# Attention and gated MLP in one kernel: two exponentials of a step joined over two PSUM banks, unit maxima turned by VectorE, other engines for small copies

## The chip, the cores and the metric

The kernel runs on one core of a Trainium2 chip. The metric is the device time of one execution in microseconds (us), lower is better. A core has TensorE (PE; its weight loads are shown apart as PEld), VectorE (DVE), ScalarE (ACT), GpSimd (POOL) and SyncE (SP, which here only issues DMAs). Matmuls write to PSUM, eight banks of 128 partitions x 512 float32.

## What is computed

Shapes: x is 2048 x 512, 32 heads of 16, the MLP has 1376 hidden columns. All is float32.

```python
xn = _layernorm(x, axis=-1)
s = _A_ref(xn, A_wqkv, A_wo)          # multi-head attention: softmax(q k^T / 4) v, then @ wo
g = _silu(_B_ref(xn, B_w1, B_b1, B_w2, B_b2))   # gelu(xn @ w1 + b1) @ w2 + b2
return x + s * g
```

## The kernel before, in words

The work is done in stages. First x is normalised and turned, V and the first of Q and K are projected (to about 60 us). Then the MLP and the other projections run (60 to 466 us). Then comes attention (466 to about 1540 us), and the output projection with the gate, which is interleaved with the last part of attention.

Attention is cut into 32 *units*, u = 4g + c: a group g of four heads and a chunk c of 512 queries. A unit has 16 *steps*, one for each block k of 128 keys. There are two kinds of score matmuls.

- **S, the scores for the row maxima** (`s_whole`, `s_op`, L185). Queries lie on the partitions, keys along 512 columns; VectorE takes maxima of each half of the bank with one reduction (`s_max`, L191, output `mx`). A unit needs 64 of these banks. A third of them is made ahead, during the MLP (`fill`, LEAD = 144 of each kind), so that attention starts with nine units of maxima in hand; in attention three are made a step.
- **T, the scores for the exponentials** (`t_one`, L715). Keys lie on the partitions, the unit's 512 queries along the columns, with two more contraction rows that carry minus the row maximum in two parts. ScalarE makes the exponential (L717, output `PT[u, k]`, one 128 x 512 block for each of the four heads). Then four matmuls of 32 columns each, in pieces that show as eight rows, multiply by V (`pv_step`, L781) into one bank, `pv`, kept through the 16 steps of the unit. L781 of step n uses the exponentials of step n - 1.

Each step issues a fixed sequence, a string in `ORDER` or `AFTER`: T is a score matmul for an exponential, S a whole bank of scores for maxima, X and Y the two halves (256 columns each) of a bank that is filled by both row halves of the array, V is L781. Before Y, PE's queue holds until the matmul of X has ended. The letter strings are chosen by the step's place k in its unit. When maxima are used up, for the last 20 steps, the string is "TTTTV", with output projection matmuls (L905) between.

Score matmuls have 48 or 50 contraction rows, so two fit on the array at once: an index `a` of 0 or 1 gives the row half (partitions 0 or 64 on). The program is in manual order: each engine works through its instructions as they were emitted. The first S of a step is on half 0, the second on half 1; X is on half 0, Y on half 1. The four T of a step have (p, a) = (0, 1), (1, 1), (0, 0), (1, 0).

PSUM: `ps_a`, `ps_b` and `ps_x` form a ring for S, X and Y (`s_tile`). T uses `ps_m` and the three rotating banks of `ps_t` (`t_tile`), `pv` has `ps_v`.

The way of the maxima of a unit: 64 reductions fill `mx`; `s_end0` reduces it with a sign change to `nm`, 128 queries x 16 (L248); Pool splits `nm` into a high and a low part (L251, L252); `s_end1` turns both, for two units together (a *pair*, up to unit 28), by a matmul with an identity into a bank (L268); `s_end2` copies that to SBUF, by ScalarE during the MLP and by VectorE later (L276, L278), and sends it to DRAM with one DMA (L279). `load_mh` brings it back as the two extra rows of Q (L153). `s_end0` is called only in the steps with k > 2 of a unit, and from unit 28 on at once. The turn follows two calls of V later in attention.

At the end of a unit, one V into the next, VectorE copies `pv` to `os` (L788) and DMAs spread it (L801, L804); division by the sum follows with Pool (L819). `pv` has one bank, so the V of the next unit's first step waits for that copy.

Of the kernel before, what the change touches and what calls it, by code (L numbers as in the profile page):

```python
# [40 lines left out]
ORDER = {0: "TTTTV", 3: "TSXTTSTYV"}  # L41
AFTER = {0: "STXTTSTYV", 2: "XTSTTYSTV"}
HC = CH // 2
PAIRED = 28
KB = 3
# [5 lines left out]
def fused(ctx: ExitStack, tc: tile.TileContext, x, wqk, wv, wo, w1, b1, w2, b2, out):  # L51
# [7 lines left out]
    ps_t = ctx.enter_context(tc.tile_pool(name="ps_t", bufs=3, space=PSUM))  # L59
# [8 lines left out]
    mh_d = dpool.tile([NG * NCH, 2, GH, CH], F32, name="mh_d")  # L68

    ident_r = keep.tile([P, P], F32R, name="ident_r")  # L70
# [16 lines left out]
    QS, QT, MX, NM, MH = {}, {}, {}, {}, {}  # L87
# [62 lines left out]
    def load_mh(u):  # L150
        assert u in sent
        for a in range(2):
            nc.sync.dma_start(QT[u][64 * a + 48:64 * a + 50].bitcast(F32), mh_d[u, :, a::2, :])  # L153
# [13 lines left out]
    def flush():  # L167
        while later and later[0][0] <= 0:
            u = later.pop(0)[1]
            run_off()  # L170
            s_end1(u)
            s_end2(u)
# [65 lines left out]
    def s_end0(u):  # L238
        ended.remove(u)
        nm = qring.tile([P, GH * NCH], F32, name="nm")  # L240
        n = len(units_of(u))
        if u == units_of(u)[0]:
            NM[u] = qring.tile([P, 2, 2, GH * NCH], F32R, name="nmh")[:, :n]
        hl = NM[units_of(u)[0]][:, u % n]
        if u == units_of(u)[-1]:
            later.append([12 if "seen" in prog else 8, units_of(u)[0]])
        mx = MX.pop(u).rearrange("p a b c n -> p (a b) (c n)")
        nc.vector.tensor_reduce(nm, mx, axis=AX.X, op=OP.max, negate=True)  # L248

        def two():  # L250
            nc.gpsimd.tensor_copy(hl[:, 0], nm)  # L251
            nc.gpsimd.tensor_sub(hl[:, 1], nm, hl[:, 0].bitcast(F32))  # L252

        put_off.append(two)
        if "seen" in prog or u == NU - 1:
            run_off()
        del QS[u]
        if "seen" in prog:
            ask_qs(u + 2)
        else:  # L260
            load_qs(u + 2)
# [3 lines left out]
    def s_end1(u):  # L265
        pm = s_tile()[0] if "seen" in prog or u == NU - 1 else t_tile()
        n = 2 * GH * NCH * len(units_of(u))
        nc.tensor.matmul(pm[:n, :P], NM.pop(u).rearrange("p u i a -> p (u i a)"), ident_r, start=True, stop=True)  # L268
        MH[u] = pm

    def s_end2(u):
        us = units_of(u)
        n = 2 * GH * NCH * len(us)
        mh = qring.tile([4 * GH * NCH, P], F32, name="mh", bufs=1)
        if "seen" in prog:
            nc.scalar.activation(mh[:n], MH.pop(u)[:n, :P], AF.Copy)  # L276
# [115 lines left out]
    with ExitStack() as s1:  # L392
# [4 lines left out]
        def a_tile(shape):  # L397
# [4 lines left out]
            return ps_t.tile(list(shape), F32, name="pst")  # L402
# [77 lines left out]
        def consts():  # L480
# [4 lines left out]
            nc.gpsimd.tensor_copy(ident_r, ident)  # L485
# [55 lines left out]
    new_k(keep_r)  # L541
    kts.append([kv[:, p] for p in range(2)])
# [17 lines left out]
    s_when, put, row = [], [0], [0]  # L560
    def fill(a):
        due = 2 * FILL0 + APART * (put[0] + sum(made))
        if sum(made) < 4 * LEAD and row[0] >= due and (made[0] <= made[1]) == (a == 0):
            taken()
            if later and later[0][0] <= 0:
                put[0] += 1
                u = later.pop(0)[1]
                s_end1(u)
                s_end2(u)
                return  # L570
# [54 lines left out]
    def down(c, f, part):  # L625
        i = c * FT + f
        if f == 0 and part == 0:
            PA[c] = [ps_v.tile([P, D], F32, name="pv")] + [ps_t.tile([P, D], F32, name="pst") for t in range(3)]
# [49 lines left out]
    def quad(n, at):  # L678
        us = first[n]
        for u, b in zip(us, BANKS[n]) if at == 0 else ():  # L680
            pool, name = {"x": (ps_x, "ps"), "m": (ps_m, "ps"), "v": (ps_v, "pv"), "t": (ps_t, "pst")}[b]
            PH[u] = pool.tile([P, CH], F32, name=name)
# [15 lines left out]
    turns, PN = [0], []  # L698

    def t_tile():  # L700
        turns[0] += 1
        if turns[0] < 5:
            pool = (ps_m, ps_x, ps_a, ps_b)[turns[0] - 1]
        else:
            pool = ps_m if turns[0] % 4 == 1 else ps_t
        return pool.tile([P, CH], F32, name="pst" if pool is ps_t else "ps")

    def t_one(u, k, p, a):
        g = u // NCH
        if (u, k) not in PT:  # L710
            PT[u, k] = slot(3 + len(PN) % 3, (P, GH, CH))
            PN.append(1)
        ps = t_tile()
# [3 lines left out]
        nc.scalar.activation(PT[u, k][:, 2 * p + a, :], ps, AF.Exp, scale=SCALE)  # L717

    k_ones(kts[0])
    for n, e in enumerate(plan):  # L720
# [6 lines left out]
        else:  # L727
            if e[1] == parts[-2]:
                nc.scalar.activation(mhw, ident_r[:1, :1].bitcast(F32), AF.Exp)
            if e[1] == parts[-1]:  # L730
                for i in range(EARLY):
                    t_one(0, 0, i // 2, i % 2)
# [42 lines left out]
    def pv_step(u, k):  # L775
# [8 lines left out]
        if k == NT - 1:  # L784
            OS[u] = wb.tile([P, CH], F32, name="os", bufs=1)
            pv = PV.pop(u)
            if u < NU - 1:
                nc.vector.tensor_copy(OS[u], pv)  # L788
# [80 lines left out]
    def w_mul(t, ks, parts=(0, 1)):  # L869
        if t not in PW:  # L870
            PW[t] = [ps_t.tile([P, CH], F32, name="pst") if NW <= t < NT - NCH or i else
# [62 lines left out]
    for u in range(NU):  # L934
# [41 lines left out]
    for n in range(L + 1):  # L976
# [78 lines left out]
```

## Time and profile before

| | before |
|---|---|
| median of 3 runs | 1565.8 us (1565.47 to 1566.19) |
| the profiled execution | 1565.5 us |
| its span, first to last instruction | 1563.7 us |
| granted TensorE clock | 1.0 throughout |
| attention, first to last start of V | 470.4 to 1541.3 us |
| maxima reductions on VectorE (L191) | 2048, 687 ns each |
| exponentials on ScalarE (L717) | 2048, 603 ns each |

A profile row gives a line of the program, an engine, an operation, what is written and read (`out<-in`, buffer numbers left out), shapes as partitions x elements, and a count. A weight load shows columns as "128*32". Rows of the timeline begin with the start in us from the span's start and the duration; neighbours of one kind are merged, with "x3" for three. Rows of the sums by stage give the stretch, its length, and for each engine the busy time and the number of instructions. Busy time of PE overlaps itself, because matmuls are pipelined: a row of 0.39 us does not hold the array for 0.39 us. Two rows of the same kind that follow each other give the better price, by the distance of their starts.

### The profile page before, as it was taken

The numbers are of one execution on the slowest core, as the hardware profiler recorded it, in microseconds if no ns is written. First come the engines' busy times: TensorE is split into PE (matmuls) and PEld (weight loads), VectorE is DVE, ScalarE is ACT, GpSimd is POOL, SyncE is SP. The second block draws the span as 40 slices with busy tenths as digits, with TensorE's granted clock in tenths as the row PEclk, the third lists the DMA queues.
The fourth block names the chain that finished last, engine by engine and source line by source line (L and its number), as shares of the span: only waits on it lengthen the run. The fifth ranks groups of instructions, "written<-read, shape, count | busy, mean of one in ns | idle before, by whom it ended". The sixth has DMA issues, their size and how long they took to land.

```text
span 1563.7 us, 31870 instructions
## 1 busy us (share of the span) xinstructions
PE 1556.6 (100%) x12264; PEld 951.5 (61%) x12264; DVE 1416.1 (91%) x2290; ACT 1234.5 (79%) x2397; POOL 371.7 (24%) x394
## 2 busy tenths in 40 slices
PE   9999999999999999999999999999999999999998
PEld 7899999999994444444444444444444444444455
DVE  7599999999999999999999999999999999999834
ACT  4333333434349999999999999999999999999984
POOL 4145575756640011001100100100010000000143
PEclk9999999999999999999999999999999999999999
DMA  6626343454322113111511411321151111110163
GB/s 209 153 60 158 116 139 100 155 145 136 124 91 60 40 42 61 29 38 44 86 24 28 70 41 32 59 44 29 26 79 27 33 29 33 40 30 22 46 197 115
DMA packets 74648, 116.87 MB, mean 75 GB/s; under 512 B 23013, under 2 KB 24293, under 8 KB 73321
## 3 DMA queue, kind: packets, MB, share of 16 engines
q1 hardware_dynamic: 70748, 101.89, 23.9%
q0 software_dynamic: 3264, 12.35, 4.7%
q8 instruction: 97, 1.59, 0.4%
q10 hardware_dynamic: 484, 0.60, 0.1%
q14 instruction: 55, 0.44, 0.1%
HBM read 84.35 MB, written 25.97 MB: 71 GB/s over the span
## 4 chain that ended last, share of the span: by engine, by line
PE 98%; DVE 1%; ACT 0%; DMA 0%; issue 0%; DVEq 0%
PE pv L781 33%; PE pst L715 20%; PE ps L589 13%; PE ps L185 11%; PE pst L589 7%; PE ps L715 7%; PE pv L589 2%; PE ps L905 1%; PE ps L82 1%; PE ps L459 1%; PE pst L82 1%; DVE st L418 0%; PE pst L441 0%; DMA xt<-in_x 0%; PE pst L459 0%; ACT slot L717 0%
## 5 line engine op out<-in xcount | busy, mean ns | idle before, releaser
L191 DVE TENSOR_REDUCE mx<-ps 128x2 f32<-128x512 f32 x2048 | 1317.9, 687 | 87.2 <-PE ps L185 44.4
L717 ACT ACTIVATE slot<-pst 128x512 f32<-128x512 f32 x1533 | 826.0, 603 | 12.8 <-PE pst L715 7.0
L781 PE MATMUL pv<-slot,vsb 128*32 128x512 f32 x4096 | 545.4, 605 | 0.3 <-DVE os L788 0.3
L715 PE MATMUL pst<-qt,kt 50*128 50x512 f32 x1149 | 378.8, 430 | 0.5 <-DVE gt L648 0.3
L185 PE MATMUL ps<-kt,slot 48*128 48x512 f32 (+1 forms) x1364 | 377.1, 368 | 0.0
L715 PEld LDWEIGHTS pst<-qt,kt 50*128 50x128 f32 x1149 | 192.3, 185 | 252.5 <-ACT slot L717 235.9
L717 ACT ACTIVATE slot<-ps 128x512 f32<-128x512 f32 x515 | 310.9, 604 | 1.8 <-PE ps L185 0.7
L185 PEld LDWEIGHTS ps<-kt,slot 48*128 48x128 f32 x1364 | 226.6, 184 | 39.4 <-DVE mx L191 35.4
L589 PE MATMUL ps<-slot,w1h 64*128 64x512 f32 x1088 | 218.4, 393 | 0.0
L185 PE MATMUL ps<-kt,qz 48*128 48x512 f32 x512 | 201.8, 394 | 0.0
L185 PE MATMUL ps<-slot,slot 48*128 48x512 f32 (+1 forms) x598 | 165.3, 366 | 0.0
L715 PE MATMUL ps<-qt,kt 50*128 50x512 f32 x387 | 160.6, 417 | 0.0
L589 PEld LDWEIGHTS ps<-slot,w1h 64*128 64x128 f32 x1088 | 151.9, 186 | 10.5
L589 PE MATMUL ps<-slot,w1l 64*128 64x512 f32 x544 | 148.4, 393 | 0.0
L781 PEld LDWEIGHTS pv<-slot,vsb 128*32 128x32 f32 x4096 | 81.0, 108 | 98.9 <-issue 90.4
L378 POOL TENSOR_TENSOR hl<-hg,hh 128x512 fp32r<-128x512 f32 x76 | 96.8, 1296 | 151.9 <-ACT hh L377 113.9
L251 POOL CAST nmh<-nm 128x16 fp32r<-128x16 f32 x32 | 6.3, 197 | 519.4 <-DVE nm L248 418.0
L371 ACT ACTIVATE hg<-ps,b_sb 128x512 f32<-128x512 f32 x44 | 27.9, 684 | 125.2 <-PE ps L589 100.4
L715 PE MATMUL pst<-qt,slot 50*128 50x512 f32 x384 | 112.5, 416 | 0.0
L185 PEld LDWEIGHTS ps<-slot,slot 48*128 48x128 f32 x598 | 99.1, 184 | 16.4 <-DVE mx L191 15.1
L715 PEld LDWEIGHTS ps<-qt,kt 50*128 50x128 f32 x387 | 71.3, 185 | 41.8 <-ACT slot L717 36.0
L185 PEld LDWEIGHTS ps<-kt,qz 48*128 48x128 f32 x512 | 94.0, 184 | 0.5
(165 smaller groups left out, 1722.6 us busy)
## 6 DMA issues: line engine op xcount, KB each, us to landing
raw<-in_w SPq DMA_DIRECT2D x88, 256.0 KB
qk_h<-hh SPq DMA_DIRECT2D x32, 256.0 KB
qk_l<-hl SPq DMA_DIRECT2D x32, 256.0 KB
qt<-qk_h SPq DMA_DIRECT2D x128, 64.0 KB
slot<-qk_h SPq DMA_DIRECT2D x92, 64.0 KB
g_d<-gt POOLq DMA_DIRECT2D x16, 256.0 KB, 3.4
qt<-qk_l SPq DMA_DIRECT2D x64, 64.0 KB
dn<-den_d SPq DMA_DIRECT2D x32, 128.0 KB
```

The source lines that it names most:

```text
L82: nc.tensor.matmul(ps, lhs[a], rhs[b], start=first and n == 0, stop=last and n == 2)
L185: return nc.tensor.matmul(ps[:, c0:c0 + w], QS[u][r, p, qi * P:(qi + 1) * P], kts[u // NCH % KB][p][r, k0:k0 + w], start=True, stop=True).ins
L191: nc.vector.tensor_reduce(MX[u][:, 2 * p:2 * p + 2, qi, ki][:, heads, parts], ps.rearrange("p (n c) -> p n c", c=HC), axis=AX.X, op=OP.max)
L251: nc.gpsimd.tensor_copy(hl[:, 0], nm)
L371: nc.scalar.activation(raw, ph.pop(u), AF.Gelu_apprx_tanh, bias=b1_sb[:, u[2]:u[2] + 1])
L378: nc.gpsimd.tensor_sub(hl, raw, hh.bitcast(F32))
L459: nc.tensor.matmul(pq["q", g, c], W1[g][i][:, k * P:(k + 1) * P], (xh, xl)[j][c][:, k], start=n == 0 and k == 0, stop=n == 2 and k == KT - 1)
L589: i = nc.tensor.matmul(ps, lhs[r], rhs[r], start=first, stop=last).ins
L715: nc.tensor.matmul(ps, kts[g % KB][p][r, k * P:(k + 1) * P], QT[u][r, p, :], start=True, stop=True)
L717: nc.scalar.activation(PT[u, k][:, 2 * p + a, :], ps, AF.Exp, scale=SCALE)
L781: nc.tensor.matmul(PV[u][32 * j:32 * j + 32, :], vsb[:, k, h:h + 32], PT[u, k][:, j, :], start=(k == 0), stop=(k == NT - 1))
L905: HALF[0] = nc.tensor.matmul(PW[i][0], OTS[i, k][x][r], (wo_h, wo_l)[y][r, k], start=k == 0 and side == 0 and n == 0, stop=k == KT - 1 and ...
```

## The change

- The four T of a step have other sides, `SIDES`: (p, a) = (1, 1), (0, 0), (0, 1), (1, 0). The banks are fixed by the place in the step: the first T has the one bank of `ps_t`, the second and third have the two banks of one tile `two_t`, the fourth has `ps_m`.
- In steps with three S the exponentials of the second and third T are one instruction over both banks, 128 x 1024 columns, after the third T. In the other steps each T keeps its own.
- Every step with three S has the order "XTSTTYSTV", which before was that of the third step of a unit alone.
- The copy of `pv` to `os` at the end of a unit is ScalarE's, except for the last unit.
- Maxima: `nm` of both units of a pair share a tile of 32 columns, cleared once by Pool. VectorE turns it in blocks of 32 x 32 (one `transpose` a pair). Pool's split follows that, once for a pair. The matmul with the identity, its bank and the copy out of it are gone. Four DMAs, one for each 32 partitions, send the result to DRAM, in pieces of 32 numbers, into a tensor with its first two indices exchanged.
- `s_end0` is called in the first four steps of a unit, and at once from unit 27 on. The due step of `load_mh` follows that. During the MLP a send no longer takes the place of an S.
- The table of exponentials is loaded with another small operand, and the copy of the identity is gone.
- Buffers of the stages before, which used `ps_t`, take the same three banks through `t_bank`.

```diff
-ORDER = {0: "TTTTV", 3: "TSXTTSTYV"}
-AFTER = {0: "STXTTSTYV", 2: "XTSTTYSTV"}
+ORDER = {0: "TTTTV", 3: "XTSTTYSTV"}
+SIDES = ((1, 1), (0, 0), (0, 1), (1, 0))
 PAIRED = 28
+DEFER = 27
...
-    ps_t = ctx.enter_context(tc.tile_pool(name="ps_t", bufs=3, space=PSUM))
+    ps_t = ctx.enter_context(tc.tile_pool(name="ps_t", bufs=1, space=PSUM))
+    ps_p = ctx.enter_context(tc.tile_pool(name="ps_p", bufs=1, space=PSUM))
...
+    two_t = ps_p.tile([P, 2, CH], F32, name="two_t")
+    spare = [0]
+
+    def t_bank(i=None):
+        if i is None:
+            i = spare[0] % 3
+            spare[0] += 1
+        return two_t[:, i] if i < 2 else ps_t.tile([P, CH], F32, name="pst")
...
     def s_end0(u):
         ended.remove(u)
-        nm = qring.tile([P, GH * NCH], F32, name="nm")
-        n = len(units_of(u))
-        if u == units_of(u)[0]:
-            NM[u] = qring.tile([P, 2, 2, GH * NCH], F32R, name="nmh")[:, :n]
-        hl = NM[units_of(u)[0]][:, u % n]
-        if u == units_of(u)[-1]:
-            later.append([12 if "seen" in prog else 8, units_of(u)[0]])
+        us = units_of(u)
+        w = u % 2 * GH * NCH
+        nm = nms[u // 2 % 2]
         mx = MX.pop(u).rearrange("p a b c n -> p (a b) (c n)")
-        nc.vector.tensor_reduce(nm, mx, axis=AX.X, op=OP.max, negate=True)
+        nc.vector.tensor_reduce(nm[:, w:w + GH * NCH], mx, axis=AX.X, op=OP.max, negate=True)
+        if u == us[-1]:
+            later.append([12 if "seen" in prog else 8, us[0]])
+            nt = qring.tile([P, 2 * GH * NCH], F32, name="nt")
+            nc.vector.transpose(nt, nm)
+            mh = MH[us[0]] = qring.tile([P, 2, 2 * GH * NCH], F32R, name="mh")
 
         def two():
-            nc.gpsimd.tensor_copy(hl[:, 0], nm)
-            nc.gpsimd.tensor_sub(hl[:, 1], nm, hl[:, 0].bitcast(F32))
+            if u == us[-1]:
+                nc.gpsimd.tensor_copy(mh[:, 0], nt)
+                nc.gpsimd.tensor_sub(mh[:, 1], nt, mh[:, 0].bitcast(F32))
...
-    def s_end1(u):
...
-    def s_end2(u):
+    def s_send(u):
         us = units_of(u)
-        n = 2 * GH * NCH * len(us)
-        mh = qring.tile([4 * GH * NCH, P], F32, name="mh", bufs=1)
-        if "seen" in prog:
-            nc.scalar.activation(mh[:n], MH.pop(u)[:n, :P], AF.Copy)
-        else:
-            nc.vector.tensor_copy(mh[:n], MH.pop(u)[:n, :P])
-        nc.sync.dma_start(mh_d[us[0]:us[-1] + 1].rearrange("u i j (q s) -> (u i j q) s", s=P), mh[:n])
+        mh = MH.pop(u)
+        n = GH * NCH
+        for b in range(4):
+            r0 = 32 * b + u % 2 * n
+            dst = mh_d[:, us[0]:us[-1] + 1].rearrange("i u j (q b s) -> b (u j q) i s", q=NCH, b=4)[b]
+            nc.sync.dma_start(dst, mh[r0:r0 + n * len(us)].bitcast(F32))
         sent.update(us)
...
-    def t_one(u, k, p, a):
+    def t_one(u, k, i, pair=False):
         g = u // NCH
+        p, a = SIDES[i]
...
-        ps = t_tile()
+        if u == k == 0:
+            ps = (ps_m, ps_x, ps_a, ps_b)[i].tile([P, CH], F32, name="ps")
+        elif i == 3:
+            ps = ps_m.tile([P, CH], F32, name="ps")
+        else:
+            ps = t_bank((i + 2) % 3)
         r = slice(64 * a, 64 * a + 3 * DH + 2)
         nc.tensor.matmul(ps, kts[g % KB][p][r, k * P:(k + 1) * P],
                          QT[u][r, p, :], start=True, stop=True)
-        nc.scalar.activation(PT[u, k][:, 2 * p + a, :], ps, AF.Exp, scale=SCALE)
+        if not pair or i in (0, 3):
+            nc.scalar.activation(PT[u, k][:, 2 * p + a, :], ps, AF.Exp, scale=SCALE)
+        elif i == 2:
+            nc.scalar.activation(PT[u, k][:, :2], two_t, AF.Exp, scale=SCALE)
...
             if u < NU - 1:
-                nc.vector.tensor_copy(OS[u], pv)
+                nc.scalar.activation(OS[u], pv, AF.Copy)
...
-            need = min(n for n in range(L) if due(n) >= 64 * (units_of(u)[-1] + 1)) + (9 if u < PAIRED else 4 if u < NU - 1 else 2)
+            last = units_of(u)[-1]
+            need = min(n for n in range(L) if due(n) >= 64 * (last + 1))
+            if last < DEFER:
+                need = min(n for n in range(need + 2, L) if n % 16 < 4)
+            need += 5 if u < PAIRED else 4 if u < NU - 1 else 2
...
-            if u >= PAIRED or ka > 2 and since.setdefault(u, n) < n:
+            if u >= DEFER or ka < 4 and since.setdefault(u, n) < n:
                 s_end0(u)
         order = ORDER[want] if n > 1 else ("TTTTV", "TTSTSVT")[n]
-        if want == 3 and ua:
-            order = AFTER.get(ka, order)
...
-                    t_one(ua, ka, i % 2, 1 - i // 2)
+                    t_one(ua, ka, i, want == 3)
```

More of the change, by code (lines that the diff above doesn't have):

```diff
@@ L170, in flush @@
             run_off()
[L171 to L172 removed]
+            s_send(u)
     def at_of(job):
@@ L541, in fused @@
     new_k(keep_r)
+    nms = [qring.tile([P, 2 * GH * NCH], F32, name=f"nm{i}", bufs=1) for i in range(2)]
+    for nm in nms:
+        nc.gpsimd.memset(nm, 0.0)
     kts.append([kv[:, p] for p in range(2)])
@@ L559, in fused @@
     writer = {}
-    s_when, put, row = [], [0], [0]
+    s_when, row = [], [0]
     def fill(a):
-        due = 2 * FILL0 + APART * (put[0] + sum(made))
+        due = 2 * FILL0 + APART * sum(made)
         if sum(made) < 4 * LEAD and row[0] >= due and (made[0] <= made[1]) == (a == 0):
@@ L627, in down @@
         if f == 0 and part == 0:
-            PA[c] = [ps_v.tile([P, D], F32, name="pv")] + [ps_t.tile([P, D], F32, name="pst") for t in range(3)]
+            PA[c] = [ps_v.tile([P, D], F32, name="pv")] + [t_bank(i) for i in (0, 2, 1)]
         h, w = HS[c, f], W2[c, f]
@@ L697, in fused @@
     PT = {}
[L698 to L706, printed above, removed]
-    def t_one(u, k, p, a):
+    PN = []
+    def t_one(u, k, i, pair=False):
         g = u // NCH
+        p, a = SIDES[i]
         if (u, k) not in PT:
@@ L728, in fused @@
             if e[1] == parts[-2]:
-                nc.scalar.activation(mhw, ident_r[:1, :1].bitcast(F32), AF.Exp)
+                nc.scalar.activation(mhw, b1_sb[:1, :1], AF.Exp)
             if e[1] == parts[-1]:
                 for i in range(EARLY):
-                    t_one(0, 0, i // 2, i % 2)
+                    t_one(0, 0, i)
             down(*e[1])
```

30 lines of the change are left out of this document (12 added, 18 removed).

## The prediction

> **What bounds the kernel now.** I read the page first, then the sums by stage, the chain of waits, and the timeline of single steps.
>
> ```profile
> PE 1556.6 (100%) x12264; PEld 951.5 (61%) x12264; DVE 1416.1 (91%) x2290; ACT 1234.5 (79%) x2397; POOL 371.7 (24%) x394
> ...
> 60.00:466.00 406.00, 406.00 (x3471) 376.18 (x3469) 391.51 (x583) 144.97 (x265) 234.82 (x207) 1.00 0.42 121
> ...
> 900.00:1300.00 400.00, 400.00 (x3122) 189.02 (x3122) 377.70 (x622) 397.38 (x780) 25.16 (x42) 1.00 0.20 40
> ...
> 473.00 1.07 PE pv L781 x8
> 1457.83 1.07 PE pv L781 x8
> ...
> 472.90:1457.70 984.80, 510.44 (x3832) 75.63 (x3832) 1.00 0.20 40
> ```
>
> In the attention stage PE, VectorE and ScalarE are all above 94% (third row, after the span: PE, PEld, DVE, ACT), so shares tell nothing and steps must be read. 3832 matmuls of the product with V, 8 a step, are 479 steps between the two rows of the chain: 984.83 us, 2.056 us a step. Nearly all that the change touches lies there. One step with the order "XTSTTYSTV", and the marks of ten regular steps after it:
>
> ```profile
> 964.12 1.06 PE L781 MATMUL pv<-slot,vsb 128*32 128x512 f32 x8
> 965.11 0.38 PE L185 MATMUL ps<-slot,slot 48*128 48x256 f32 x1
> 965.11 0.50 PE L715 MATMUL pst<-qt,kt 50*128 50x512 f32 x1
> 965.34 0.43 PE L185 MATMUL ps<-slot,slot 48*128 48x512 f32 x1
> 965.46 0.39 PE L715 MATMUL pst<-qt,kt 50*128 50x512 f32 x1
> 965.61 0.39 PE L715 MATMUL ps<-qt,kt 50*128 50x512 f32 x1
> 965.69 0.68 PE L185 MATMUL ps<-slot,slot 48*128 48x256 f32 x2
> 965.88 0.49 PE L715 MATMUL pst<-qt,kt 50*128 50x512 f32 x1
> 966.30 1.07 PE L781 MATMUL pv<-slot,vsb 128*32 128x512 f32 x8
> ...
> 986.66 1.07 PE L781 MATMUL pv<-slot,vsb 128*32 128x512 f32 x8
> ```
>
> V holds PE for 0.99 us (964.12 to 965.11). After it a matmul of 512 columns costs its row half 0.23 us (T1 at 965.46, Y at 965.69 on the same half), one of 256 columns 0.12 us, and the first 0.12 us more (T0 to T1 takes 0.35). The ten steps from 966.30 to 986.66 take 2.036 us each, this one 2.18. By those prices a step walks through in 0.12 + 3 x 0.23 + 0.12, some 0.08 until V starts, and 0.99: 2.00 us. So PE alone sets all but 0.03 us of a regular step. The 0.03 comes from two deadlines that are met just in time:
>
> ```profile
> 973.14 0.68 DVE L191 TENSOR_REDUCE mx<-ps 128x2 f32<-128x512 f32 x1
> 973.35 0.62 ACT L717 ACTIVATE slot<-pst 128x512 f32<-128x512 f32 x1
> 973.38 0.50 PE L715 MATMUL pst<-qt,kt 50*128 50x512 f32 x1
> ...
> 973.88 0.18 PEld L185 LDWEIGHTS ps<-slot,slot 48*128 48x128 f32 x1
> 974.02 0.18 PEld L715 LDWEIGHTS pst<-qt,kt 50*128 50x128 f32 x1
> ```
>
> This step starts at 973.38. VectorE's last maximum of the step before ends at 973.82, and the weights of the second S load 0.06 later, 0.50 into the step; by the walk that S starts at 0.58. ScalarE's last exponential of the step before ends at 973.97, and T3's weights load 0.05 later, 0.64 in; T3's place is 0.70.
>
> **The change, part by part.** Prices of single instructions (count, then least, median and largest ns, in the rows with a colon):
>
> ```profile
> L717 ACT ACTIVATE slot<-pst x1533: 589/599/698, 469.9 to 1539.9; 128x512 f32<-128x512 f32 x192
> L276 ACT ACTIVATE mh<-ps x4: 270/270/272, 157.0 to 429.4; 64x128 f32<-64x128 f32 x4
> 901.93 1.57 ACT L717 ACTIVATE slot<-pst 128x512 f32<-128x512 f32 x3
> ...
> 661.91 1.28 DVE L191 TENSOR_REDUCE mx<-ps 128x2 f32<-128x512 f32 x2
> 965.80 1.29 DVE L191 TENSOR_REDUCE mx<-ps 128x2 f32<-128x512 f32 x2
> ...
> L788 DVE COPY os<-pv 128x512 f32<-128x512 f32 x31 | 21.1, 681 | 0.0
> L373 ACT ACTIVATE hg<-ps 128x512 f32<-128x512 f32 x30 | 16.6, 596 | 63.0 <-PE ps L589 56.9 <-PE ps L459 6.1
> L248 DVE TENSOR_REDUCE nm<-mx x32: 273/276/288, 104.4 to 1479.9; 128x16 f32<-128x128 f32 x32
> L419 DVE BATCH_NORM_AGGREGATE mv<-st 128x2 f32<-128x6 f32 x16 | 2.9, 182 | 0.6
> ```
>
> *Joined exponential.* Three in a row take 1.57 us, so one follows the other after 0.48. No row has 1024 columns. From 128 to 512 columns an activation grows by 599 - 270 = 329 ns, 0.857 ns a column; 512 more columns make 1.04 us, followed after 0.91. Two single ones cost 0.96, so ScalarE saves 0.05 us a step. Bounds: no more than 0.6 for the pair (gain 0.36), no less than nothing, and a loss of 0.1 if reading over two banks stalls. I take 0.91, since the slope is measured on the same source and engine. The Trainium skill (ScalarE: Activation LUTs, What ACT_TABLE_LOAD costs) gives 186 ns + 0.833 ns per column and 93 ns of overlap. Its slope agrees with the rows, its overlap does not (0.60 - 0.48 = 0.12). By the page the pair saves 0.09, and the sum below would be some 3 us lower.
>
> *Order and sides.* Row half 0 now runs X, S, T1, T3, row half 1 runs T0, T2, Y, S: each 256 + 3 x 512 columns, as before. By the same prices T2 starts at 0.35, Y at 0.58, the second S and T3 at 0.70, V at 1.01: no cost, if T2 may start while T1, ahead of it in the program, still waits for its half. That matmuls of the two halves pass each other is seen near the end, where T0 and T1 (both half 1) stand ahead of L905 (half 0):
>
> ```profile
> 1498.54 0.49 PE L715 MATMUL pst<-qt,kt 50*128 50x512 f32 x1
> 1498.54 0.50 PE L905 MATMUL ps<-wo_h,oh 64*128 64x512 f32 x1
> 1498.87 0.39 PE L715 MATMUL pst<-qt,kt 50*128 50x512 f32 x1
> ```
>
> L905 started with T0, 0.33 before T1.
>
> *The two deadlines.* VectorE: first maximum at 0.69 (965.80 after 965.11), two intervals of 0.60 (1.28 - 0.68), 0.68 to the end, 0.06 to the load: 2.63, which is 0.60 into the next step; the second S has moved from 0.58 to 0.70. Its slack stays about nothing: 0.10 ahead of its place now against 0.08. The bank it waits for is always that of the second S before, since the ring of three turns so in this order. ScalarE: T0's 0.50, start at 0.53, then 0.48, 0.91, 0.61 and 0.05: T3's bank is free at 2.58, 0.55 into the next step instead of 0.64, for a place at 0.70. So one of two tight deadlines loosens by 0.09. I take half of the 0.03 away, a step of 2.025 (both ends below): 479 x (2.025 - 2.036) = **-5.3 us**.
>
> *Copy of a unit's output* (os) from VectorE to ScalarE. Now it makes the third step of a unit 2.18 instead of 2.036, 0.145 late, 30 times: -4.4. On ScalarE it takes 0.48 of the stream (L373's kind) where a step leaves 2.03 - (0.48 + 0.91 + 0.48) = 0.16: the next step's exponentials run 0.32 late and T3's bank comes at 0.87 instead of by 0.62, 0.25 late, after which the spare time has caught up: 30 x 0.25 = +7.5. Between 0 and 0.48 a unit; net **+3.1 us**, since what is copied ends only after V, behind the last exponential.
>
> *Turning the maxima.* TensorE's transposes go:
>
> ```profile
> 873.50 1.06 PE L781 MATMUL pv<-slot,vsb 128*32 128x512 f32 x8
> 874.50 0.28 PE L268 MATMUL ps<-ident_r,nmh 128*64 128x128 f32 x1
> 875.78 1.06 PE L781 MATMUL pv<-slot,vsb 128*32 128x512 f32 x8
> ...
> 60.00:466.00 406.00, 1.10 (x4) 0.53 (x4) 1.00 0.42 121
> 466.00:1480.00 1014.00, 3.49 (x13) 1.65 (x13) 1.00 0.20 42
> ```
>
> A step with one takes 2.28, 0.24 more than 2.036; 17 and one later: 18 x 0.24 = **-4.3 us**. The four in the first stage count in full, as PE has no gap there. VectorE gets a block transpose of 128 x 32 a pair, 0.18 (L419) to 0.28 (L248); 0.24 taken, 0.16 of its stream, behind the maximum of maxima (0.28, 0.20 of the stream). A step leaves VectorE 2.03 - 3 x 0.60 = 0.23, so the pair is 0.13 late at the second S: 14 x 0.13 = **+1.8 us** (0 to 14 x 0.25). What waits behind both on VectorE is the first maximum of that step.
>
> *Maxima later, four DMAs instead of one.* Pool's two operations stay. The pieces shrink to 128 bytes and SP issues three more DMAs a pair; behind them on SP stand the loads of Q and the moves of outputs, which have many steps in hand, and the maxima themselves are loaded 5 steps after their deferred point and at least 5 steps (10 us) before the unit that reads them, 3 long ones for the last unit. Nothing; if that cover went, PE would stall once for a pair by a DMA's few us. The identity copy, memsets and renamed banks: nothing, off every deadline.
>
> **Sum:** -5.3 + 3.1 - 4.3 + 1.8 = -4.7, on the profiled execution's 1565.5 (span 1563.7): 1560.8. The median shown is 0.3 above that execution, so **1561**. Own range 1554 to 1564.
>
> **Rivals.**
> 1. *The second S becomes the wait (slower).* VectorE's deadline closes a loop: from X to the first maximum, two intervals, the end, the load 2.63 in all; from that load to V 0.43 where it came late (the second of the two at 965.69 ends at 966.37, and begins 0.50 before, 965.87; V at 966.30); V 0.99. Twice the step is then 4.05, a step of 2.025, just the forecast. It decides from there on: each 0.07 us that the first maximum comes later adds 0.035 a step. At 2.06: 479 x 0.024 = +11.5, +0.6 from the other terms: 1578. For: the slack is nothing. Against: the regular steps now lie on the same edge.
> 2. *T2 waits for T1.* Half 1 then idles from 0.35 to 0.47 in each step, 479 x 0.12 = +57: 1623. Against: L905 passing T1 above. The Trainium skill (PSUM — Partial Sum Buffer, Engine vs sequencer instructions) says that matmuls start and complete in program order; by that rule this rival holds, and the rows at 1498.54 speak against it for two row halves.
> 3. *The regular step stays at 2.036*, the edge of VectorE alone keeping it: +0.6, 1566. For: that edge does not loosen.
> 4. *Both hide.* Steps of 2.010 and the copy free: -12.5 - 4.4 - 4.3 = -21: 1545. For: the walk of 2.00.
> 5. *The join saves nothing*, 1.08 in the stream: T3's bank at 0.72 is 0.10 late, half of that a step in the same kind of loop, 2.06 and more: 1580.
>
> **How the numbers follow.** Forecast 0.44 (0.40 of it faster, 0.04 within 0.2%); rival 1 0.20, 2 0.04, 3 0.17 (0.14 within, 0.03 slower), 4 0.09, 5 0.06. A measurement here tells 0.2%, 3 us, from no change. Faster 0.40 + 0.09 = 0.49; same 0.18; slower 0.33. The range 1546 to 1581 leaves out rival 2, half of 4 and the upper tail of 1 and 5.
>
> **What would show it.** Right: regular steps near 2.025; the joined activation near 1.04 us; the step with its weights for the second S loaded near 0.60; a long step once a unit, two after the os copy, ended by ScalarE; no step of 2.28. Wrong: Y starting at 0.70 (rival 2); second S later than 0.75 in most steps (rival 1); a joined activation of 1.2 us; units of 16 steps no shorter than 32.9.

## The result and the profile after

The changed kernel takes **1592.28 us** (median of 4 runs, 1588.11 to 1594.03) against 1565.9 us before (median of 4 runs, 1565.47 to 1566.19): a ratio of 1.0164, with a 95% interval of 1.0152 to 1.0176. It is 26 us slower; the forecast was 1561 us, and 1592 lies outside its range of 1546 to 1581. The profiled execution took 1591.91 us with a span of 1589.2 us.

Whole steps are counted best from the first matmul of each product with V (L781 before, L788 after; 512 of them, numbered from 1). The span then falls into five stretches. All the experiments, which are told further down, are in the same table (the last column has medians, the others the profiled execution; the stretches leave out step 490 itself, some 2 us, so they add to a little less than the span):

| kernel (us) | to the first V | steps 1 to 10 | steps 10 to 490 | from step 491 to the end | span | median of the runs |
|---|---|---|---|---|---|---|
| before | 470.4 | 18.9 | 987.0 | 85.4 | 1563.7 | 1565.9 |
| after | 486.1 | 21.4 | 979.4 | 100.3 | 1589.2 | 1592.3 |
| tail joined | 488.0 | 21.4 | 979.3 | 84.9 | 1575.6 | 1577.1 |
| early banks apart | 472.6 | 22.1 | 979.5 | 101.2 | 1577.4 | 1578.1 |
| both | 471.9 | 21.4 | 979.3 | 84.7 | 1559.3 | 1560.9 |
| both, tail banks apart and not joined | 471.9 | 21.4 | 979.4 | 84.7 | 1559.4 | 1561.2 |
| both, handover mended | 470.2 | 22.0 | 979.5 | 84.8 | 1558.6 | 1559.9 |
| both, os on VectorE | 471.6 | 19.9 | 984.1 | 85.5 | 1563.1 | 1567.0 |
| both, os split | 473.0 | 20.9 | 988.4 | 84.9 | 1569.2 | 1570.8 |
| both, old order | 472.7 | 22.1 | 983.5 | 85.0 | 1565.3 | 1565.2 |
| before, new order | 471.3 | 18.9 | 990.2 | 85.1 | 1567.5 | 1569.1 |
| before, os on ScalarE | 471.0 | 18.9 | 994.5 | 84.8 | 1571.3 | 1573.4 |

After minus before is +15.7, +2.5, -7.6 and +14.9. The steps on which the forecast spent its working did become faster, by 3 us more than it said. The loss lies in three places that it had passed over with one sentence.

**The first loss: layer norm and its transposes.** The MLP's first matmul starts at 51.7 us before and at 65.5 us after, 13.8 later. First the transposes of one round in the timeline before, where eight fill two banks one after the other without a wait:

```profile
10.32 1.07 PE L441 MATMUL pst<-ident,xn 128*128 128x128 f32 x8
```

From the timeline of the changed kernel, the columns being start, duration, engine, line, operation, tiles, and in brackets the idle time of the engine and what ended it; first TensorE:

```profile
10.33 0.62 PE L446 MATMUL two_t<-ident,xn 128*128 128x128 f32 x4
12.65 0.65 PE L446 MATMUL two_t<-ident,xn 128*128 128x128 f32 x4 [1.70 <-DVE slot L78]
...
23.99 0.66 PE L446 MATMUL two_t<-ident,xn 128*128 128x128 f32 x4 [2.61 <-DVE slot L78]
...
36.58 1.11 PE L446 MATMUL two_t<-ident,xn 128*128 128x128 f32 x4 [2.72 <-DVE slot L78]
...
50.49 1.12 PE L446 MATMUL two_t<-ident,xn 128*128 128x128 f32 x4 [2.56 <-DVE slot L78]
```

and VectorE in the same stretch:

```profile
10.70 1.29 DVE L78 TENSOR_TENSOR slot<-ps,slot 128x512 fp32r<-128x512 f32 x2
11.91 0.68 DVE L78 TENSOR_TENSOR slot<-two_t,slot 128x512 fp32r<-128x512 f32 x1
13.97 0.69 DVE L78 TENSOR_TENSOR slot<-two_t,slot 128x512 fp32r<-128x512 f32 x1 [1.38 <-ACT slot L77]
```

Four transposes fill one bank of `two_t` from 10.33. The next four, for the other bank, start only at 12.65, right after VectorE's reading of the first bank ends (11.91 + 0.68 = 12.59). Nothing was in the other bank. The three banks were turns of one ring before; now two of them are the halves of one tile, and the program orders accesses to that tile as if they met. It happens once in each of four rounds, 9.6 us of waits in all. With the third and the fourth the granted clock also falls to a half, for 3.4 us each in the trace. The sums by stretch show the first of these drops (the last three numbers are the granted clock, the DMA share and GB/s):

```profile
36.00:40.00 4.00, 3.42 (x13) 3.09 (x14) 2.00 (x4) 1.20 (x2) 0.77 (x1) 0.57 0.63 197
```

**The second loss: the last twenty steps**, 3.06 us each before, 3.86 after. One of them before, with the third T (T2; the four are T0 to T3) at 1.81 us from the start of V:

```profile
1500.61 1.07 PE L781 MATMUL pv<-slot,vsb 128*32 128x512 f32 x8
...
1502.42 0.40 PE L715 MATMUL pst<-qt,kt 50*128 50x512 f32 x1
...
1503.68 1.06 PE L781 MATMUL pv<-slot,vsb 128*32 128x512 f32 x8
```

One in the timeline of the changed kernel, with T2 at 2.73 us:

```profile
1516.39 1.06 PE L788 MATMUL pv<-slot,vsb 128*32 128x512 f32 x8
...
1517.39 0.49 PE L719 MATMUL two_t<-qt,kt 50*128 50x512 f32 x1
...
1518.48 0.59 ACT L722 ACTIVATE slot<-two_t 128x512 f32<-128x512 f32 x1
1519.12 0.18 PEld L719 LDWEIGHTS two_t<-qt,kt 50*128 50x128 f32 x1 [0.96 <-ACT slot L722]
1519.12 0.49 PE L719 MATMUL two_t<-qt,kt 50*128 50x512 f32 x1 [0.52 <-ACT slot L722]
...
1520.25 1.06 PE L788 MATMUL pv<-slot,vsb 128*32 128x512 f32 x8
```

These steps have no S (`want` is 0), so `t_one` gets `pair` false and makes four single exponentials. T1 writes one half of `two_t` at 1517.39. T2, for the other half, waits until T1's exponential has been read out (1518.48 + 0.59 = 1519.07). Here T2 stands in the path that sets the end, since its own exponential and T3's still follow before V.

**The third loss: the handover to attention.** The starts of the last MLP matmul and the first V stood 1.95 us apart before and 3.96 after. TensorE had one short wait there before:

```profile
469.36 0.49 PE L715 MATMUL pst<-qt,kt 50*128 50x512 f32 x1 [0.31 <-DVE gt L648]
```

TensorE in the changed kernel's timeline:

```profile
483.01 0.50 PE L719 MATMUL pst<-qt,kt 50*128 50x512 f32 x1 [0.52 <-DVE gt L651]
484.21 0.50 PE L719 MATMUL two_t<-qt,kt 50*128 50x512 f32 x1 [0.70 <-DVE gt L651]
...
485.39 0.50 PE L719 MATMUL two_t<-qt,kt 50*128 50x512 f32 x1 [0.46 <-ACT slot L722]
...
489.44 1.93 PE L788 MATMUL pv<-slot,vsb 128*32 128x512 f32 x8
```

It waits for VectorE's additions (`gt`), which read the MLP's banks, and then (485.39) for one half's single exponential before it writes the other half. Right after it, the product with V takes 1.93 us instead of 1.06: the granted clock is 0.50 in the stretch from 488 to 492 us, and the first nine steps take 21.4 us instead of 18.9.

**The gain: the regular step.** The changed kernel's timeline over three steps, the second of them with the copy of a unit's output:

```profile
974.39 1.07 PE L788 MATMUL pv<-slot,vsb 128*32 128x512 f32 x8
974.40 1.02 ACT L724 ACTIVATE slot<-two_t 128x1024 f32<-128x1024 f32 x1
975.31 0.61 ACT L722 ACTIVATE slot<-ps 128x512 f32<-128x512 f32 x1
...
975.72 0.51 PE L719 MATMUL two_t<-qt,kt 50*128 50x512 f32 x2
...
975.96 0.51 PE L194 MATMUL ps<-slot,slot 48*128 48x256 f32 x2
...
976.40 1.06 PE L788 MATMUL pv<-slot,vsb 128*32 128x512 f32 x8
...
977.79 0.62 ACT L795 ACTIVATE os<-pv 128x512 f32<-128x512 f32 x1
977.84 0.28 DVE L253 TENSOR_REDUCE nm<-mx 128x16 f32<-128x128 f32 x1
...
978.22 0.21 DVE L257 STREAM_TRANSPOSE nt<-nm 128x32 f32<-128x32 f32 x1
...
978.46 1.07 PE L788 MATMUL pv<-slot,vsb 128*32 128x512 f32 x8
978.75 1.07 ACT L724 ACTIVATE slot<-two_t 128x1024 f32<-128x1024 f32 x1
...
979.87 0.19 PEld L719 LDWEIGHTS two_t<-qt,kt 50*128 50x128 f32 x2
...
980.36 0.18 PEld L719 LDWEIGHTS ps<-qt,kt 50*128 50x128 f32 x1
...
980.78 0.16 PEld L788 LDWEIGHTS pv<-slot,vsb 128*32 128x32 f32 x8 [0.24 <-issue]
```

The joined activation is followed after 0.91 us, T1 and T2 start 0.11 us apart (975.72 and 975.84 in the trace, one row here), and V follows V in 2.01 us (974.39 to 976.40). The os copy makes the next two steps 2.06 and 2.32 us; they are called the os steps below. In the second, the joined activation ends only at 979.82, and the loads for its two banks come at 979.87, 0.41 into the step (from 979.46, where the array is free of V), where those of a regular step come at 0.20.

### The profile page after: what moved, and what is told of

Same layout as the page of the kernel before. It is cut to its first block, busy times and chain, and to the rows that moved or that the text cites. A ratio compares the mean times of both kernels' runs of the same rounds, so it can differ in the third digit from the quotient of the medians.

```text
span 1589.2 us, 31354 instructions
## 1 busy us (share of the span) xinstructions
PE 1560.8 (98%) x12246; PEld 930.6 (59%) x12246; DVE 1399.2 (88%) x2263; ACT 1226.9 (77%) x1934; POOL 366.8 (23%) x367
## 4 chain that ended last, share of the span: by engine, by line
PE 95%; ACT 3%; DVE 1%; issue 0%; DMA 0%; ACTq 0%; DVEq 0%
PE pv L788 32%; PE ps L194 21%; PE ps L592 12%; PE two_t L719 8%; PE two_t L592 5%; PE ps L719 5%; PE pst L719 4%; PE pst L592 2%; PE pv L592 2%; ACT slot L722 2%; PE ps L464 1%; PE ps L83 1%; PE ps L912 1%; ACT slot L724 1%; PE two_t L83 0%; DVE slot L78 0%
## 5 line engine op out<-in xcount | busy, mean ns | idle before, releaser
L788 PE MATMUL pv<-slot,vsb 128*32 128x512 f32 x4096 | 546.5, 606 | 0.0
L724 ACT ACTIVATE slot<-two_t 128x1024 f32<-128x1024 f32 x490 | 503.3, 1027 | 0.1
L194 PEld LDWEIGHTS ps<-kt,slot 48*128 48x128 f32 x1364 | 213.4, 184 | 296.5 <-DVE mx L200 286.0
L194 PE MATMUL ps<-kt,slot 48*128 48x256 f32 (+1 forms) x1364 | 373.4, 362 | 0.0
L722 ACT ACTIVATE slot<-pst 128x512 f32<-128x512 f32 x511 | 308.6, 604 | 19.3 <-PE two_t L719 7.0
L719 PE MATMUL two_t<-qt,kt 50*128 50x512 f32 x766 | 206.8, 405 | 11.7 <-ACT slot L722 11.0
L719 PE MATMUL pst<-qt,kt 50*128 50x512 f32 x383 | 190.4, 497 | 0.5 <-DVE gt L651 0.5
L194 PE MATMUL ps<-slot,slot 48*128 48x256 f32 (+1 forms) x598 | 164.6, 364 | 0.0
L592 PE MATMUL ps<-slot,w1l 64*128 64x512 f32 x544 | 160.8, 392 | 0.0
L788 PEld LDWEIGHTS pv<-slot,vsb 128*32 128x32 f32 x4096 | 80.8, 108 | 131.7 <-issue 122.9
L719 PEld LDWEIGHTS two_t<-qt,kt 50*128 50x128 f32 x766 | 112.9, 186 | 23.8 <-ACT slot L722 20.1
L826 POOL TENSOR_TENSOR slot<-slot,dn 64x512 f32<-64x512 f32 x16 | 20.5, 1281 | 332.0 <-DMA dn<-den_d 117.7
```

Source lines behind the costliest of these rows:

```text
L194: return nc.tensor.matmul(ps[:, c0:c0 + w], QS[u][r, p, qi * P:(qi + 1) * P], kts[u // NCH % KB][p][r, k0:k0 + w], start=True, stop=True).ins
L592: i = nc.tensor.matmul(ps, lhs[r], rhs[r], start=first, stop=last).ins
L719: nc.tensor.matmul(ps, kts[g % KB][p][r, k * P:(k + 1) * P], QT[u][r, p, :], start=True, stop=True)
L724: nc.scalar.activation(PT[u, k][:, :2], two_t, AF.Exp, scale=SCALE)
L788: nc.tensor.matmul(PV[u][32 * j:32 * j + 32, :], vsb[:, k, h:h + 32], PT[u, k][:, j, :], start=(k == 0), stop=(k == NT - 1))
L826: eng.tensor_mul(ot[c][rs, g // 2], ot[c][rs, g // 2], DN.pop(u)[rs])
```

## The experiments

The theory from the two traces: the two banks in one tile are ordered as one, and that alone makes the early stage and the tail slow; everything else in the change is a gain of some 5 to 8 us. The rivals: the new order or the copy on ScalarE costs more than the join brings, and the tail is late because its single exponentials follow the joined ones.

**Tail joined.** The join is used in all steps from the third on:

```diff
-                    t_one(ua, ka, i, want == 3)
+                    t_one(ua, ka, i, n > 1)
```

> The changed kernel, with the middle exponentials joined also in the last 20 steps of attention (those without S). Theory: there the third T waits for the single exponential of the second T, because both banks belong to one tile; joined, no exponential stands between the two. The last steps go from 3.86 to 3.06 us, the stretch from step 491 to the end from 102.3 back to 85.4 us, the time from 1592.3 to about 1575 us. Rival: these steps are long because maxima or gate data arrive later; then they stay at 3.86 and the time at 1592.

1577.1 us (1576.71 to 1577.56), 1.0072 of before (1.0058 to 1.0086). The tail goes from 100.3 to 84.9 us and its steps back to 3.05. One activation that reads both halves leaves nothing to wait for between them. Steps 1 to 490 stay; the first V is 1.9 us later, with three drops of the clock in the first stage instead of two.

**Early banks apart.** Until attention three separate banks turn, and the double tile is made only then:

```diff
+    p3 = ExitStack()
+    ps_3 = p3.enter_context(tc.tile_pool(name="ps_3", bufs=3, space=PSUM))
...
     def t_bank(i=None):
-        if i is None:
-            i = spare[0] % 3
-            spare[0] += 1
-        return two_t[:, i] if i < 2 else ps_t.tile([P, CH], F32, name="pst")
+        if not late_t:
+            return ps_3.tile([P, CH], F32, name="pst")
+        return late_t[1][:, i] if i < 2 else late_t[0].tile([P, CH], F32, name="pst")
...
+    p3.close()
+    late_t.append(ctx.enter_context(tc.tile_pool(name="ps_t", bufs=1, space=PSUM)))
+    late_t.append(ctx.enter_context(tc.tile_pool(name="ps_p", bufs=1, space=PSUM)).tile([P, 2, CH], F32, name="two_t"))
```

> The changed kernel, with three separate rotating banks until attention begins, and the two-bank tile made only then. Theory: before the MLP a matmul into one bank of the tile waits for the reading of the other; with separate banks the MLP's first matmul comes back from 65.5 to 51.7 us, and the handover to attention may lose its 2 us: 1592.3 - 13.8 = 1578.5, or 1576.5. Rival: the start is later because of the missing identity copy, other Pool work or the lower granted clock; then nothing moves, 1592.

1578.06 us (1576.87 to 1579.13), 1.0078 (1.0064 to 1.0092). The first V comes 13.5 us earlier, at 472.6. The sum over the first 60 us in this kernel:

```profile
0.00:60.00 60.00, 58.16 (x336) 49.01 (x338) 34.10 (x87) 25.80 (x50) 22.08 (x30) 1.00 0.69 196
```

TensorE is busy 58.16 of 60 us (48.84 in the changed kernel) and the clock is full again. The handover isn't mended by this: the last MLP matmul and the first V stand 4.9 us apart, and steps 1 to 10 take 22.1 us.

**Both.** The two edits together:

> Both edits together. Theory: the two losses add and nothing else of the change is slower than before: 1592.3 - 16.9 - 13.8 = 1561.6, 1559.6 with the handover, faster than before by 0.3 to 0.4%. Rival: the steps of attention gain because they are fed by a later start (maxima in hand, other phase); then attention is no shorter than before and the time is 1566 or more.

1560.87 us (1559.45 to 1563.0), 0.9969 (0.9958 to 0.998): faster than before by 5 us, and near the 1561 us forecast for a change whose renamed banks cost nothing. The two edits bring 14.2 and 15.2 us alone and 31.4 together, so the losses add, as far as the spread of the changed kernel (1588 to 1594) lets one say. That the time is so near the forecast is partly luck: by the table attention gains 7.7 us and the tail 0.7, while the way to the first V and steps 1 to 10 still lose 1.5 and 2.5.

**Both, tail banks apart and not joined.** Joining the tail removes the wait and two activations at once, so it doesn't tell whether the shared tile or the single exponentials were to blame. Here the tail keeps its four single exponentials, and the double tile is given up for three turning banks at the first step without an S:

```diff
+    def tail_banks():
+        lp.close()
+        late_t.clear()
+        tail_t.append(ctx.enter_context(tc.tile_pool(name="ps_4", bufs=3, space=PSUM)))
...
     def t_bank(i=None):
+        if tail_t:
+            return tail_t[0].tile([P, CH], F32, name="pst")
...
+        if n > 1 and want == 0 and not tail_t:
+            tail_banks()
```

> This is the kernel of the run with separate early banks and a tail of single exponentials on the double tile (1578.1 us); the tile of two banks is given up at the first of the last steps without an S, and the T's of the tail take three separate banks in turn, still with four single exponentials a step. Theory (the two banks in one tile are ordered as one, and that alone made the tail late): the last twenty steps go back to 3.06 us each from 3.86, and 15 to 17 us come back: 1560.5 to 1563 us. Rival (single exponentials behind joined ones, or the new order of the steps, make the tail late): 1576 to 1579 us, steps of 3.8 us.

1561.17 us (1560.59 to 1561.86), 0.9972 (0.9961 to 0.9983); the tail is 84.7 us. The same place of the timeline in this kernel:

```profile
1508.80 1.06 PE L800 MATMUL pv<-slot,vsb 128*32 128x512 f32 x8
...
1510.33 1.58 ACT L731 ACTIVATE slot<-pst 128x512 f32<-128x512 f32 x3 [0.47 <-PE pst L728]
...
1510.84 0.39 PE L728 MATMUL pst<-qt,kt 50*128 50x512 f32 x1
...
1511.85 1.06 PE L800 MATMUL pv<-slot,vsb 128*32 128x512 f32 x8
```

The third T starts at 1510.84, while the first of the three exponentials from 1510.33 still runs (the three end at 1511.91), and the step takes 3.05 us. The rival falls: single exponentials in the new order cost nothing in the tail; the shared tile did.

**Both, handover mended.** The second step joins too, and there the first T and the last one change banks:

```diff
-        elif i == 3:
+        elif i == (0 if (u, k) == (0, 1) else 3):
             ps = ps_m.tile([P, CH], F32, name="ps")
         else:
-            ps = t_bank((i + 2) % 3)
+            ps = t_bank((2, 0, 1, 2)[i])
...
-                    t_one(ua, ka, i, n > 1)
+                    t_one(ua, ka, i, n > 0)
```

> This is the kernel of the run with separate early banks and a joined tail (1560.9 us), with two more edits at the start of attention: the step n = 1 joins its middle exponentials too, and its first T and last T change banks, so that the first T no longer waits for a bank that VectorE still reads from the MLP stage. Theory: in that run TensorE stands idle 1.8 us and then 0.9 us there, and the granted clock drops to 0.5 for 6.8 us right after; with the idle time gone, 2 to 2.5 us come back, with the clock kept at 1.00 some 1.5 to 2 us more: 1556 to 1558.5 us, no row with a clock under 0.9 in the first 20 us of attention. Rival: the clock drop comes from the change of stage itself and stays, and only the waits go: 1558.5 to 1560. Second rival: the first V takes the wait on instead: 1560 to 1562.

1559.88 us (1556.96 to 1560.39), 0.9958 (0.9945 to 0.997): the best of all, by 1 us, though its interval overlaps that of the kernel without the edit. The clock, from this kernel's timeline and its sums by stretch:

```profile
469.54 0.50 PE L717 MATMUL two_t<-qt,kt 50*128 50x512 f32 x2 [1.46 <-DVE gt L649]
...
470.20 1.94 PE L789 MATMUL pv<-slot,vsb 128*32 128x512 f32 x8
```

```profile
470.00:474.00 4.00, 3.53 (x16) 1.15 (x14) 1.29 (x2) 1.62 (x2) 0.32 (x1) 0.53 0.62 231
```

The second wait is gone and the first V comes 1.7 us earlier (2.8 us behind the last MLP matmul, where it was 4.5); the first, for VectorE's additions, still leaves 1.46 us of idle time, the clock falls to half as it did, and steps 1 to 10 give 0.6 of the gain back. So for this execution, and by the median, the first rival of that run, a clock drop that stays, is nearest. But of the five executions two have a mean granted clock of 1.000, and these took 1557.71 and 1556.96 us, as the theory forecast; the other three, at 0.997 and 0.998, took 1559.9 to 1560.4. So the change of stage doesn't always bring the drop, and the drop is worth some 3 us. None of the seven executions of the kernel without the edit had a mean clock above 0.999. Before, with an idle time of 0.31 us at this place, the clock stayed at 1.00.

**Both, os on VectorE.** The copy of a unit's output goes back to the engine that had it:

```diff
-                nc.scalar.activation(OS[u], pv, AF.Copy)
+                nc.vector.tensor_copy(OS[u], pv)
```

> Both edits, and the copy of a unit's output back on VectorE. In the changed kernel the two steps after that copy are long (2.07 and 2.32 against 2.014), 0.32 us a unit, 9.5 us in all. Theory: ScalarE's copy makes the fourth T late. On VectorE the copy takes 0.60 of a stream with 0.23 to spare, so the second S comes up to 0.37 late: the long step moves to another wait and the time stays within 3 us of the run before. Rival: it costs 0.145 a unit as it did before the change: 5 us less.

1567.02 us (1564.79 to 1568.14), 1.0006 (0.9997 to 1.0015): the whole gain is lost, 6 us by the medians and 3.8 by the spans, more than either side had expected. (The span hides some of it, as the clock was at half for 3.4 us at this kernel's handover and for 6.8 in the run before it; from step 10 to the end this kernel takes 5.6 us longer.) The two long steps of a unit take 2.17 + 2.22 us where VectorE has only the copy, 2.17 + 2.41 where it also has the maximum of maxima, and 2.17 + 2.70 where the block transpose comes too; on ScalarE they are 2.06 + 2.32 in all three. So in a unit without maxima in these steps the copy costs the same on either engine. VectorE and TensorE in such a step, from this kernel's timeline:

```profile
701.52 0.68 DVE L796 COPY os<-pv 128x512 f32<-128x512 f32 x1
702.12 0.28 DVE L251 TENSOR_REDUCE nm<-mx 128x16 f32<-128x128 f32 x1
702.50 0.21 DVE L255 STREAM_TRANSPOSE nt<-nm 128x32 f32<-128x32 f32 x1
702.63 3.73 DVE L198 TENSOR_REDUCE mx<-ps 128x2 f32<-128x512 f32 x6
```

```profile
702.25 1.06 PE L789 MATMUL pv<-slot,vsb 128*32 128x512 f32 x8
...
704.95 1.06 PE L789 MATMUL pv<-slot,vsb 128*32 128x512 f32 x8
```

The change puts the maxima into a unit's first four steps, just where the copy is. 0.60 + 0.38 + 0.13 us on VectorE, start to start, stand ahead of the maxima that free the S banks. Neither edit can be priced without the other.

**Both, os split.** 256 columns to each of the two engines:

```diff
-                nc.scalar.activation(OS[u], pv, AF.Copy)
+                nc.scalar.activation(OS[u][:, :HC], pv[:, :HC], AF.Copy)
+                nc.vector.tensor_copy(OS[u][:, HC:], pv[:, HC:])
```

> As e3_both, with the copy of a unit's output cut in two: 256 columns by ScalarE, 256 by VectorE. Theory: a half takes some 0.26 of ScalarE's stream (0.16 to spare) and 0.33 of VectorE's (0.21 to spare), so the long steps shrink from 0.32 to about 0.1 us a unit: 6 to 7 us less than e3_both, 1554. Rival: both halves lie in one bank, so VectorE's half waits for ScalarE's and holds up VectorE's queue: no better than e3_both, 1561 to 1567.

1570.82 us (1569.39 to 1572.02), 1.0032 (1.002 to 1.0043): slower than either side had expected. The halves run one after the other, in this kernel's timeline:

```profile
573.31 0.41 ACT L796 ACTIVATE os<-pv 128x256 f32<-128x256 f32 x1
...
573.75 0.42 DVE L797 COPY os<-pv 128x256 f32<-128x256 f32 x1 [0.32 <-ACT os L796]
...
574.23 1.06 PE L789 MATMUL pv<-slot,vsb 128*32 128x512 f32 x8 [0.23 <-DVE os L797]
```

VectorE waits 0.32 us for ScalarE's half (573.31 + 0.41 = 573.72), though the two take different columns. V then waits for VectorE. Both halves read one bank, and both write one tile, `os`; this run doesn't show which of the two orders them. The Trainium skill (PSUM — Partial Sum Buffer, PSUM bank collisions raise a hardware error) asks that accesses of different engines to one bank be kept apart; the order seen here agrees with it. The same rule, bank by bank, doesn't ask for the wait between the two banks of `two_t`, which cost some 30 us with the clock drops behind it (1592.3 against 1560.9).

**Both, old order.** The steps keep "TSXTTSTYV" instead of "XTSTTYSTV":

> As e3_both, with the order TSXTTSTYV of before in every step with three S. In e3_both the regular step takes 2.014 us, before the change 2.036. Theory: the joined exponential loosened ScalarE's deadline for the fourth T, and that is what the 0.022 came from; then the old order also runs at 2.014, within 2 us of e3_both's 1560.9. Rival: the new order loosened VectorE's deadline for the second S; then the regular step is 2.036 again, 479 x 0.022 = 10.5 us more, 1571.

1565.21 us (1564.38 to 1567.07), 0.9998 (0.9989 to 1.0007). The regular step is 2.025 us, between 2.036 before and 2.014: neither side was right. The join brings about half, together with the new sides, which this run keeps; the order brings the other half. The sides have no run of their own.

**Before, new order.** The kernel before, with "XTSTTYSTV" in every step and no exceptions after it (`AFTER` empty):

> The kernel before, with the order XTSTTYSTV in all steps with three S and nothing else. Theory (ScalarE's deadline limits the regular step, and four single exponentials keep it tight): the regular step stays near 2.036, 1566 within 2 us. Rival (VectorE's deadline, which the order moves): 2.014 and 1555.

1569.08 us (1568.85 to 1569.87), 1.0022 (1.0014 to 1.0031). Three regular steps in its timeline, from V to V:

```profile
706.79 1.07 PE L781 MATMUL pv<-slot,vsb 128*32 128x512 f32 x8
...
708.86 1.06 PE L781 MATMUL pv<-slot,vsb 128*32 128x512 f32 x8
...
710.87 1.06 PE L781 MATMUL pv<-slot,vsb 128*32 128x512 f32 x8
...
712.93 1.07 PE L781 MATMUL pv<-slot,vsb 128*32 128x512 f32 x8
```

They take 2.07 and 2.01 us in turn, much as before (medians 2.06 and 2.02). The order by itself, with the old sides, brings nothing; only with the join and the new sides does it level the steps at 2.014. Its os steps are dearer (2.14 and 2.23 against 2.06 and 2.19), which over 30 units is about the 3 us that it loses.

**Before, os on ScalarE.** The copy alone is moved:

> The kernel before, with the copy of a unit's output on ScalarE and nothing else. Theory: with four single exponentials a step leaves ScalarE only 0.11 us, the copy's 0.48 puts the exponentials 0.37 late, and the unit loses 0.3 to 0.4 us in place of the 0.145 of VectorE's copy: 5 to 8 us more than before, 1571 to 1574. Rival: the copy is as cheap on ScalarE as on VectorE: 1566.

1573.38 us (1573.07 to 1573.85), 1.005 (1.0034 to 1.0065). The os steps go from 2.06 and 2.19 to 2.12 and 2.39. Alone this edit loses 7.6 us, within the theory's 5 to 8, where with the rest of the change it saves.

## Why the prediction was wrong

**The step that failed** is the last half sentence of the working: "renamed banks: nothing, off every deadline". It looked at deadlines of the steady step only, where both halves of the new tile are read by one activation. It didn't ask at the other users of those banks (the transposes of layer norm, the first steps, the twenty steps without S) what the next matmul into the tile has to wait for when a half is read alone. There the ring of three turning banks had become a ring of two. By the table that is +15.7 and +2.5 us up to step 10 and +14.9 in the tail. With the early stage and the tail mended, 1.5 and 2.5 us of the handover stay, and the kernel stands at 1560.9.

**The rivals** all looked at the steady step too, and none came true: the second S didn't become the wait (in regular steps its weights load at 0.58 and its matmul starts at 0.69, its place in the forecast's walk), the regular step neither stayed at 2.036 nor lost by the join. Rival 2 had Y at 0.70 into the step, for a T2 held up by T1; Y starts at 0.57 (975.96 after 975.39), the forecast's place for a T2 that passes T1. The step of rival 4, 2.010, was nearly reached with 2.014, but the copy did not hide.

**The other terms**, against what the runs show:

- Regular step 2.025, forecast -5.3 us: measured 2.014, or 479 x (2.014 - 2.036) = -10.5 us. The join, with the new sides, gave what was forecast (2.025 in the old order); the new order, put at no cost, brings as much again on top of them.
- Joined activation of 1.04 us, followed after 0.91: measured 1.027 on average, followed after 0.91. Right. The page of the changed kernel:

```profile
L724 ACT ACTIVATE slot<-two_t 128x1024 f32<-128x1024 f32 x490 | 503.3, 1027 | 0.1
```

- Os copy, net +3.1: in the whole change two steps of 2.064 and 2.321 (medians) against 2.058 and 2.187 before. Over their regular steps that is 0.36 against 0.17 a unit, 30 x 0.19 = +5.7. The mechanism was right (T3's load at 0.87 into the step was forecast, it comes at 980.36 - 979.46 = 0.90), but T1 and T2, whose shared bank pair is freed at one time, come late too, at 0.41. And the comparison was with a VectorE that had no other new work in these steps, which isn't this kernel.
- TensorE's transposes, -4.3: the steps of 2.28 that held one are gone. The four in the MLP stage were to bring 1.0 us: from its first to its last matmul that stage took 416.74 us before and 416.62 after, but 415.3 to 415.9 in the kernels with the early banks apart. So about as much came as was forecast, and in the changed kernel it was lost again; the other edits in that stage aren't separated from it.
- Maximum of maxima and block transpose, +1.8: the transpose takes 0.21 us where 0.24 was taken. The two together hold VectorE for 0.51 us from start to start (977.84 to 978.35), where 0.36 was taken, and still cost nothing on the path, as the os steps with them and without them both take 2.32. They hide in a step that ScalarE makes long anyway.

With 14 x 0.24 = 3.4 us for the transposes in attention the terms add up to -10.5 + 5.7 - 3.4 = -8.2, where the trace shows -7.6 over steps 10 to 490. The sum for the steady part was off by a few us in several terms of both signs; the sign of the whole was lost elsewhere.

What stays open: why the clock falls at the handover in most executions and not in all, and whether a handover without any idle time would always keep it.

## What to carry to other kernels

When two buffers are made into one tile, look up every user of either, not only the one that wants them joined: whoever reads or writes a half alone is now ordered against the other half, and a ring of three has become a ring of two. Keep such a tile to the stage whose accesses take it whole, and give the banks back to a ring elsewhere. Two edits on the same engine and in the same step (here the copy and the maxima) have one price together; moved alone, this copy lost 7.6 us, and with the other edits it saved 5 to 6.

## What the runs showed of the hardware beyond that

Short gaps of TensorE were followed in some places by a clock of one half, for 3.4, 6.8 or 10.2 us in the traces. In the changed kernel waits of 0.52, 0.70 and 0.46 us within 2.9 us, and in the kernel with the handover mended a single wait of 1.46 us, stand ahead of stretches with a granted clock of 0.50 and 0.53, where V takes 1.93 us instead of 1.06. With 0.31 us at the same place, before, it stayed at 1.00. The length of a gap alone doesn't decide: in the first stage of the changed kernel no drop came behind the waits of 1.70 and 2.61 us, while one came with those of 2.72 and 2.56; with the tail joined, the same wait of 1.70 us had one behind it. What decides isn't shown. The Trainium skill (TensorE: Matmul & The Clock Gate, Why this matters for your kernels) warns of gaps of more than about 3 us; here less than 2 us in all came before a drop.
